# Local attention heads on full PE rows, two raw buffers instead of three, two more ring slots

## The chip, the cores and the metric

One core of one Trainium2 chip runs the whole program in one launch. The metric is device time in microseconds (us) of one execution. The engines are PE (TensorE; PEld is its weight load), DVE (VectorE), ACT (ScalarE), POOL (GpSimd) and SP (SyncE, which here only issues transfers). Three runs of the kernel before took 451.62, 452.07 and 452.42 us, median 452.07.

## The reference

Three layers follow each other. Attention has 4 batches of 8 heads, 576 tokens and 64 features a head. Heads 0 to 3 are local: a token sees itself and the 31 tokens before it. Heads 4 to 7 are strided: a token sees the earlier tokens that have the same remainder by 32. Then come a soft mixture of 8 experts with 4 slots each, and an MLP with a squared ReLU.

```python
rel = pos[:, None] - pos[None, :]
mask_local = (rel >= 0) & (rel < 32)
mask_strided = (rel >= 0) & (pos[None, :] % 32 == pos[:, None] % 32)
scores = where(mask, q @ k.T / 8, -1e9)          # softmax over keys, then @ v
logits = x @ phi                                 # x: 2304 x 512, phi: 512 x 32
slot_input = softmax(logits, axis=0).T @ x       # 32 slots
slot_out[e] = relu(slot_input[e] @ w1[e]) @ w2[e]
x = softmax(logits, axis=1) @ slot_out
out = relu(x @ w_in) ** 2 @ w_out                # 512 -> 2048 -> 512
```

`w_in` and `w_out` arrive with 8 bytes a number and are narrowed on the chip; everything else is f32.

## The kernel before

Attention runs in 16 units. A unit is two heads of one batch, and the order is `(b, p) for p in (0, 2, 1, 3)`, so that even units are local and odd units are strided. A step `u` of the loop works on several units at once: the transposes of q and k for unit u+1 (`Tk0 Tk1 Tq0 Tq1`, function `st_T`), the scores of unit u (`S`, `st_S`), exp (`E`) and the normalization of strided rows (`N`), the transposes of the probabilities of unit u-1 (`PT0 PT1`), its product with v (`A`, `st_AV`), the transposes of the result of unit u-2 (`X0 X1`), and for each batch the logits (`L`) and the slot sums (`R1 Rs R2 R3`). `PIPE` lists the order of these parts, one list for even steps and one for odd ones. Within the loop `pin` chains the instructions of PE, ACT, DVE and POOL in exactly this order, each engine by itself.

The raw q and k of a unit lie with 72 partitions. For a local unit `st_T` turns them with ordinary matmuls against the identity, 64 columns at a time, the two heads side by side in the PE array (`tile_position` (0, 0) and (0, 64)); for a strided unit it uses PE transposes of 128 columns. An eviction by ACT writes the turned q and k to `qTb` and `kTb`. Local scores take 18 blocks of 32 queries. Each block is one matmul for each head against 64 keys, head 0 on array rows 0 to 63 and head 1 on rows 64 to 127, in four groups of 32 columns. `st_AV` does the same for 20 blocks against v, 65 columns wide (the last column holds ones and gives the denominators). An f32 matmul stands in the trace as two PE instructions, a transpose as one. A second copy of v, moved down by 32 tokens, is made on the chip by `shift_v` (`vd` on DVE, `va` on ACT).

All transfers are issued by SP in one order (`load_to`). `NR` = 3 pairs of raw buffers hold q and k, so step u loads unit u+4 (`ld`); v of local units has two buffers (`lv` loads unit u+3). At the end of a step `ft` fetches two blocks of 512 KB of weights. These go to `RING` = 26 ring slots of 512 KB or, when an attention buffer has been given back (`give`), to one of the `NA` = 17 slots of the attention space (`space`). After the last step all slots are filled, and the experts' two layers (`layer1`, `layer2`) free them one by one. The MLP reads its own weights through the same ring.

Of the kernel before, what the change touches and what calls it, by code (L numbers as in the profile page):

```python
# [7 lines left out]
F32 = mybir.dt.float32  # L8
# [11 lines left out]
RING = 26  # L20
NA = 17
# [10 lines left out]
PAD = 0  # L32

@with_exitstack
def kernel(
# [271 lines left out]
    NR = 3  # L307
# [10 lines left out]
    for u in (NU - 2, NU - 1):  # L318
        qTb[u % 2], kTb[u % 2] = part(128, S), part(128, 32 + S)
# [7 lines left out]
    vS, Ps, Ts = part(128, 2, 8, D), part(128, 8, 2, 64), part(128, 8, 2, 36)  # L327
# [6 lines left out]
    def local(u):  # L334
        return units[u][1] < 2
# [16 lines left out]


    def pad(ps, n=PAD):
        for _ in range(n):
            nc.tensor.matmul(out=ps[:, 384:512], lhsT=identb, rhs=identb, start=True, stop=True)

    def shift_v(u, h, copy):
        vL = vLb[u // 2 % 2]
        copy(vL[64 * h:64 * h + 32, 1:18, 0:D], vL[64 * h + 32:64 * h + 64, 0:17, 0:D])  # L360

    def load_v(u):
# [3 lines left out]
        for h in range(2):  # L366
            src = v[b, 2 * p + h]
            if local(u):
                load_to(
                    vLb[u // 2 % 2][64 * h + 32:64 * h + 64, :, 0:D], src.rearrange("(j p) d -> p j d", p=32)  # L370
# [25 lines left out]
    load(2)  # L396
    load_to(phi_sb, phi.rearrange("(k p) s -> p k s", p=128))
    load_v(1)
    load_v(2)
# [8 lines left out]
    nc.vector.memset(kTb[0][:, 0:32], 0.0)  # L408
    diag(ident, [[-1, 128]], 0, 1.0)
    for vL in vLb:  # L410
        nc.vector.memset(vL[:, :, D:D + 1], 1.0)
        for h in range(2):
            nc.vector.memset(vL[ts(2 * h, 32), 0, 0:D], 0.0)
# [26 lines left out]
    behind(nc.gpsimd.memset(Ps, 0.0), last_diag)  # L440
# [5 lines left out]
    def st_T(u, which, halves=(0, 1)):  # L446
# [6 lines left out]
        for i in halves:  # L453
            ps = psum("t")
            if u:
                pad(ps)
            ps = ps[:, 0:288]
            for r in range(4):
                if not local(u):
                    nc.tensor.transpose(  # L460
                        out=ps[:, ts(r, 72)], in_=src[:, ts(4 * i + r, 128)], identity=ident[0:72, 0:72]
                    )
                    continue
                for h in range(2):
                    nc.tensor.matmul(  # L465
                        out=ps[ts(h, 64), ts(r, 72)], lhsT=src[:, ts(8 * h + 4 * i + r, 64)],
                        rhs=ident[0:72, 0:72], start=True, stop=True, tile_position=(0, 64 * h),
                    )
            if local(u):
                o = dst[:, 32 * which:32 * which + S].rearrange("c (p r) -> c p r", r=8)[:, :, ts(i, 4)]  # L470
                ps = ps.rearrange("c (r p) -> c p r", r=4)
            else:
                o = dst[:, ts(i, 288)]
            dve = u == 0 and i
            if which:
                ins = (nc.vector.tensor_copy if dve else nc.scalar.copy)(out=o, in_=ps)  # L476
            elif dve:
                ins = nc.vector.tensor_scalar(out=o, in0=ps, scalar1=scale, scalar2=None, op0=ALU.mult)
            else:
                ins = nc.scalar.activation(out=o, in_=ps, func=AF.Copy, scale=scale)  # L480
            if dve:
                v_first[0] = ins
# [13 lines left out]
    def st_S(u):  # L496
        qT, kT = qTs[u], kTb[u % 2]
        pss = [psum("s") for _ in range(2)]
        m = maskl.rearrange("p t w -> p (t w)") if local(u) else masks.rearrange("p n w -> p (n w)")
        n = m.shape[1]  # L500
        pad(pss[0])
# [796 lines left out]
```

## Time and profile before

| | us |
|---|---|
| median of three runs | 452.07 |
| the profiled execution | 451.3 |
| its span in the profile | 449.5 |
| PE busy | 408.5 (91%) |
| DVE busy | 252.5 (56%) |
| ACT busy | 242.0 (54%) |
| POOL busy | 62.5 (14%) |
| transfers, share of 16 DMA engines | 48.9% of the span |

[...] The span has three stages: attention from 0 to about 152 us with its last steps up to 177, the experts from there to about 214, and the MLP up to the end. The 1.8 us between the profiled execution's time and its span lie outside the instructions.

### The profile page before, as it was taken

Reading aid. Unit: us, or ns where it says so; the run is one execution under the profiler, and the core shown is the slowest. Engines: PE = TensorE matmul, PEld = TensorE weight load, DVE = VectorE, ACT = ScalarE, POOL = GpSimd, SP = SyncE. Lnnn points to the kernel's source line nnn. Section 1 sums busy time; section 2 is a strip of 40 time slices with the busy share of each in tenths; the row PEclk is TensorE's granted clock in tenths of the full one; section 3 lists DMA queues with packets and bytes.
Section 4 is the critical chain, followed back from the end, with each engine's and each line's share of the span. In section 5 each row is a group of like instructions: output and inputs, shape, how many; then the busy total and the mean of one; then the engine's idle time right before and its main releaser. Section 6 shows DMA issues by size and latency. Waiting matters only on the chain.

```text
span 449.5 us, 11728 instructions
## 1 busy us (share of the span) xinstructions
PE 408.5 (91%) x4910; PEld 316.0 (70%) x4910; DVE 252.5 (56%) x538; ACT 242.0 (54%) x532; POOL 62.5 (14%) x85
## 2 busy tenths in 40 slices
PE   7698886998788869999799998999999999999996
PEld 4677764676577555354577886888878888888884
DVE  4344554667445635311677667686867768635344
ACT  1334535265344512101688777766777677766660
POOL 3210100001101000000143114310242113300000
PEclk9999969698978958999999999999999999999999
DMA  7998668399845499999931223231200000003033
GB/s 149 197 215 247 178 189 236 112 253 240 226 153 190 148 412 359 365 410 408 362 97 50 92 93 93 71 117 49 93 0 1 0 2 0 1 1 141 23 117 141
DMA packets 31988, 70.02 MB, mean 156 GB/s; under 512 B 12608, under 2 KB 12864, under 8 KB 31936
## 3 DMA queue, kind: packets, MB, share of 16 engines
q1 hardware_dynamic: 31936, 69.28, 48.9%
q8 instruction: 38, 0.62, 0.6%
q14 instruction: 14, 0.11, 0.1%
HBM read 64.55 MB, written 4.72 MB: 154 GB/s over the span
## 4 chain that ended last, share of the span: by engine, by line
PE 74%; DMA 8%; DVE 7%; issue 5%; ACT 4%; POOL 1%; SPq 0%; DVEq 0%; POOLq 0%; ACTq 0%
PE t L1245 14%; PE s L1245 14%; PE o L1245 13%; DMA w<-in_moe_w_dram 5%; PE t L465 4%; PE t L1201 3%; PE o L617 3%; PE t L460 2%; PE o L786 2%; PE t L578 2%; DMA w<-in_moe_w_out_dram 2%; DMA space<-in_v_dram 2%; PE s L509 2%; PE s L523 2%; PE t L648 2%
## 5 line engine op out<-in xcount | busy, mean ns | idle before, releaser
L1222 DVE TENSOR_TENSOR w<-r,w 128x384 fp32r<-128x384 f32 x95 | 55.4, 583 | 71.8 <-ACT w L1208 71.0
L1245 PE MATMUL s<-w 128*128 128x512 f32 x288 | 83.0, 397 | 0.2 <-DVE part L1260 0.2
L1245 PE MATMUL t<-w 128*128 128x512 f32 x288 | 74.4, 393 | 0.0
L1245 PE MATMUL o<-w 128*128 128x512 f32 x288 | 73.7, 391 | 0.0
L1206 ACT ACTIVATE r<-t 128x384 f32<-128x384 f32 x94 | 46.2, 491 | 42.7 <-PE t L1201 36.7
L1245 PEld LDWEIGHTS o<-w 128*128 128x128 f32 x288 | 54.1, 188 | 12.4
L1245 PEld LDWEIGHTS s<-w 128*128 128x128 f32 x288 | 52.6, 188 | 11.6 <-ACT w L1097 0.6
L1245 PEld LDWEIGHTS t<-w 128*128 128x128 f32 x288 | 53.2, 188 | 10.3
L1207 ACT ACTIVATE r<-r 128x384 f32<-128x384 f32 x94 | 49.5, 526 | 2.9
L1208 ACT CAST w<-r 128x384 fp32r<-128x384 f32 x94 | 48.3, 514 | 3.5
L476 ACT COPY space<-t 128x288 f32<-128x288 f32 x31 | 11.7, 398 | 48.9 <-PE t L465 27.9
L190 POOL TENSOR_SCALAR nm<-w 128x512 f32<-128x512 f32 x28 | 21.2, 762 | 106.2 <-DMA w<-in_moe_w_out_dram 67.7
L1201 PE MATMUL t<-cT,A 128*128 128x384 f32 x96 | 32.3, 338 | 3.1 <-POOL A L1149 1.6
L1098 POOL TENSOR_TENSOR w<-wf,w 128x512 fp32r<-128x512 f32 x16 | 21.7, 1359 | 74.6 <-ACT w L1097 69.7
L465 PE MATMUL t<-ident,space 72*64 72x72 f32 x512 | 28.5, 288 | 1.6 <-DVE xNb L668 0.7
L465 PEld LDWEIGHTS t<-ident,space 72*64 72x64 f32 x512 | 25.6, 189 | 4.8 <-DVE xNb L668 1.9
L554 POOL TENSOR_TENSOR space<-space,sm 128x576 f32<-128x576 f32 x7 | 8.1, 1153 | 120.9 <-DVE sm L553 61.8
L193 DVE TENSOR_SCALAR nm<-nm 128x512 uint32<-128x512 uint32 x32 | 14.4, 449 | 16.8 <-ACT nm L188 10.2
L1201 PEld LDWEIGHTS t<-cT,A 128*128 128x128 f32 x96 | 17.9, 188 | 7.7 <-POOL A L1149 2.0
L194 DVE SCALAR_TENSOR_TENSOR nm<-w,nm 128x512 uint32<-128x512 uint32 x32 | 22.2, 692 | 1.1
L489 DVE TENSOR_REDUCE mx<-s 128x5 f32<-128x320 f32 (+1 forms) x32 | 15.0, 467 | 12.4 <-PE s L523 8.7
L523 PE MATMUL s<-space 64*36 64x36 f32 x512 | 9.0, 229 | 7.9 <-issue 7.9
(203 smaller groups left out, 564.8 us busy)
## 6 DMA issues: line engine op xcount, KB each, us to landing
w<-in_moe_w_dram SPq DMA_DIRECT2D x46, 512.0 KB
space<-in_moe_w_dram SPq DMA_DIRECT2D x18, 512.0 KB
w<-in_moe_w_in_dram SPq DMA_DIRECT2D x16, 512.0 KB
w<-in_moe_w_out_dram SPq DMA_DIRECT2D x16, 512.0 KB
space<-in_k_dram SPq DMA_DIRECT2D x16, 288.0 KB
space<-in_q_dram SPq DMA_DIRECT2D x16, 288.0 KB
out_dram<-part SPq DMA_DIRECT2D x17, 256.0 KB
space<-in_v_dram SPq DMA_DIRECT2D x16, 144.0 KB
```

The lines of the kernel that those rows point to most:

```text
L190: nc.gpsimd.tensor_scalar(out=m, in0=hf, scalar1=2.0 ** -112, scalar2=1.0, op0=ALU.mult, op1=ALU.mult)
L194: nc.vector.scalar_tensor_tensor(out=r, in0=hi, scalar=0x80000000, in1=r, op0=ALU.bitwise_and, op1=ALU.bitwise_or)
L465: nc.tensor.matmul(out=ps[ts(h, 64), ts(r, 72)], lhsT=src[:, ts(8 * h + 4 * i + r, 64)], rhs=ident[0:72, 0:72], start=True, stop=True, til ...
L489: nc.vector.tensor_reduce(out=mx[:, 0:n], in_=ps, axis=AX.X, op=ALU.max, negate=True)
L523: nc.tensor.matmul(out=pss[a][64 * h:64 * h + 36, ts(i, 36)], lhsT=qv[ts(a, 64), i, h], rhs=kv[ts(a, 64), i, h], start=False, stop=(i == 7 ...
L1098: nc.gpsimd.tensor_tensor(out=lo, in0=r, in1=hi.bitcast(F32), op=ALU.subtract)
L1201: nc.tensor.matmul(out=ps[:, 0:HB], lhsT=A4[c][:, ts(f % QF, 128)], rhs=cT4[:, c0:c0 + HB], start=True, stop=True)
L1206: nc.scalar.activation(out=r, in_=ps[:, 0:HB], func=AF.Relu)
L1207: nc.scalar.activation(out=r, in_=r, func=AF.Square)
L1208: nc.scalar.copy(out=gh, in_=r)
L1222: nc.vector.tensor_tensor(out=gl, in0=r, in1=gh.bitcast(F32), op=ALU.subtract)
L1245: nc.tensor.matmul(out=acc[t], lhsT=a[:, ts(t, 128)], rhs=wo[f][:, ts(w, 512)], start=(first and k == 0), stop=(last and k == 2),)
```

## The change

`st_T` treats local units like strided ones: PE transposes of 128 columns, which hold a pair of neighbouring tokens of one head, 4 for each half (a half is now a head). The result has even tokens on partitions 0 to 63 and odd ones on 64 to 127, so each half is evicted with two instructions of 64 partitions. For local units `kTb` becomes 128 x 2 x 608: head 0's keys stand on partitions 0 to 63 of the first plane, head 1's on 64 to 127 of the second, and the rest is zero. One matmul per block then computes both heads over all 128 rows, 128 columns wide; `vL` is laid out in the same way, so that `st_AV` needs one matmul of 130 columns per block. The two PSUM tiles of S and A now hold blocks of tokens (0 to 2 and 3 to 4 of five) instead of heads. `S` moves behind `Tk0 Tk1` in both lists. `vL` has one buffer instead of two, `Ts` shares the memory of `Tl`, `NR` is 2, `NA` is 15 and `RING` is 28. Local v is loaded by `load_v(a1 + 2)` in place of `a1 + 4`.

```diff
-RING = 26
-NA = 17
+RING = 28
+NA = 15
-    "Rs S Tk0 Tk1 X0 X1 PT0 PT1 Tq0 Tq1 ld E R2 A lv R3 vd va cv ft".split(),
-    "S Tk0 Tk1 L X0 X1 PT0 E PT1 N Tq0 Tq1 ld R1 A lv ft".split(),
+    "Rs Tk0 Tk1 S X0 X1 PT0 PT1 Tq0 Tq1 ld E R2 A lv R3 vd va cv ft".split(),
+    "Tk0 Tk1 S L X0 X1 PT0 E PT1 N Tq0 Tq1 ld R1 A lv ft".split(),
-    NR = 3
+    NR = 2
-            vLb = [part(128, 18, 65) for _ in range(2)]
-            Pl, Tl = part(128, 5, 2, 64), part(128, 5, 128)
+            vL, Pl = part(128, 18, 2, 65), part(128, 5, 2, 64)
...
     load(0)
     load(1)
     load_v(0)
-    load(2)
     load_to(phi_sb, phi.rearrange("(k p) s -> p k s", p=128))
     load_v(1)
-    load_v(2)
...
+    for t in (vL[0:64, :, 1, :], vL[64:128, :, 0, :], Ps):
+        behind(nc.gpsimd.memset(t, 0.0), last_diag)
...
             for r in range(4):
-                if not local(u):
-                    nc.tensor.transpose(
-                        out=ps[:, ts(r, 72)], in_=src[:, ts(4 * i + r, 128)], identity=ident[0:72, 0:72]
-                    )
-                    continue
-                for h in range(2):
-                    nc.tensor.matmul(
-                        out=ps[ts(h, 64), ts(r, 72)], lhsT=src[:, ts(8 * h + 4 * i + r, 64)],
-                        rhs=ident[0:72, 0:72], start=True, stop=True, tile_position=(0, 64 * h),
-                    )
+                nc.tensor.transpose(
+                    out=ps[:, ts(r, 72)], in_=src[:, ts(4 * i + r, 128)], identity=ident[0:72, 0:72]
+                )
             if local(u):
+                o = dst[:, i, 32:32 + S] if which else dst
+                o = o[ts(i, 64)].rearrange("c (p r a) -> c a p r", r=4, a=2)
+                io = [(ps[ts(a, 64)].rearrange("c (r p) -> c p r", r=4), o[:, a]) for a in range(2)]
...
-                for h in range(2):
-                    nc.tensor.matmul(
-                        out=pss[h][ts(cg, 32), ts(t, 64)],
-                        lhsT=qT[ts(h, 64), ts(qb, 32)], rhs=kT[ts(h, 64), 32 * qb:32 * qb + 64],
-                        start=False, stop=(qb + 4 >= 18), tile_position=(64 * h, 32 * cg),
-                    )
+                i = t >= 3
+                nc.tensor.matmul(
+                    out=pss[i][ts(cg, 32), ts(t - 3 * i, 128)].rearrange("p (h w) -> p h w", h=2),
+                    lhsT=qT[:, ts(qb, 32)], rhs=kT[:, :, 32 * qb:32 * qb + 64],
+                    start=False, stop=(t == 2 or qb + 4 >= 18), tile_position=(0, 32 * cg),
+                )
...
-                for h in range(2):
-                    nc.tensor.matmul(
-                        out=pss[h][ts(cg, 32), ts(t, 65)],
-                        lhsT=T[ts(h, 64), t, ts(cg, 32)], rhs=vL[ts(h, 64), min(qb, 17)],
-                        start=True, stop=True, tile_position=(64 * h, 32 * cg),
-                    )
+                i = t >= 3
+                nc.tensor.matmul(
+                    out=pss[i][ts(cg, 32), ts(t - 3 * i, 130)],
+                    lhsT=T[:, t, ts(cg, 32)], rhs=vL[:, min(qb, 17)].rearrange("p h e -> p (h e)"),
+                    start=True, stop=True, tile_position=(0, 32 * cg),
+                )
```

## Rows read from the trace of the kernel before

**Rows 1.** Windows by stage; PEclk is the granted clock, DMA share follows it.

```profile
core 0: us, PE busy (x) PEld busy (x) DVE busy (x) ACT busy (x) POOL busy (x), PEclk, DMA share, GB/s
...
28.13:48.11 19.98, 18.80 (x393) 15.96 (x388) 10.44 (x24) 8.88 (x20) 1.11 (x1) 1.00 0.83 199
...
89.39:104.58 15.19, 13.00 (x432) 10.76 (x427) 11.10 (x27) 8.64 (x22) 1.95 (x2) 1.00 0.96 254
...
152.34:214.00 61.66, 54.79 (x746) 31.14 (x745) 21.76 (x61) 11.16 (x29) 0.64 (x1) 0.89 0.98 384
214.00:449.50 235.50, 227.01 (x1118) 184.80 (x1118) 151.46 (x271) 163.24 (x333) 47.13 (x49) 1.00 0.21 73
...
28.13:142.31 114.18, 98.00 (x2487) 78.70 (x2481) 63.48 (x154) 53.33 (x137) 5.77 (x5) 0.87 0.75 199
```

**Rows 2.** PE's waits from 0 to 142.31 us: total, times, longest.

```profile
PE s L523 <- issue: 7.9, 4, 3.3
PE o L605 <- issue: 3.7, 3, 2.1
PE o L786 <- ACT nm L188: 3.0, 1, 3.0
...
PE t L460 <- issue: 1.8, 1, 1.8
...
PE s L509 <- issue: 0.9, 2, 0.5
```

**Rows 3.** The page: busy time and instructions of each engine; the instruction-loading queue.

```profile
PE 408.5 (91%) x4910; PEld 316.0 (70%) x4910; DVE 252.5 (56%) x538; ACT 242.0 (54%) x532; POOL 62.5 (14%) x85
...
q8 instruction: 38, 0.62, 0.6%
```

**Rows 4.** PE's timeline, parts at the lower clock: start, duration, line.

```profile
44.65 2.19 PE L465 MATMUL t<-ident,space 72*64 72x72 f32 x32
46.77 1.41 PE L605 MATMUL o<-space 64*32 64x65 f32 x80
...
48.75 1.34 PE L509 MATMUL s<-space 64*32 64x64 f32 x72
...
129.24 1.17 PE L460 MATMUL t<-ident,space 72*128 72x72 f32 x8
```

**Rows 5.** PE's timeline, the same parts at the higher clock.

```profile
52.25 0.67 PE L460 MATMUL t<-ident,space 72*128 72x72 f32 x8
...
88.41 1.04 PE L605 MATMUL o<-space 64*32 64x65 f32 x80
...
119.04 1.22 PE L465 MATMUL t<-ident,space 72*64 72x72 f32 x32
...
123.76 0.97 PE L509 MATMUL s<-space 64*32 64x64 f32 x72
```

**Rows 6.** PE's timeline, logits of two units at the lower clock.

```profile
61.34 0.63 PE L682 MATMUL t<-space,phi_sb 128*32 128x128 f32 x5
...
61.98 0.63 PE L682 MATMUL t<-space,phi_sb 128*32 128x128 f32 x5
```

**Rows 7.** Timeline of the first unit: v's issue, its shift, the scores.

```profile
2.51 0.90 SPq L115 DMA_DIRECT2D space<-in_v_dram  x2
...
10.69 1.10 ACT L360 COPY space<-space 32x1088 f32<-32x1088 f32 x1 [4.18 <-DMA space<-in_v_dram]
...
11.69 0.39 ACT L480 ACTIVATE space<-t 128x288 f32<-128x288 f32 x1
12.14 1.34 PE L509 MATMUL s<-space 64*32 64x64 f32 x72 [2.50 <-ACT space L480]
```

**Rows 8.** An odd step at the higher clock: Tq's wait.

```profile
102.17 0.72 PE L465 MATMUL t<-ident,space 72*64 72x72 f32 x16 [0.69 <-DVE xNb L668]
```

**Rows 9.** The page: ACT's evictions of turned k.

```profile
L476 ACT COPY space<-t 128x288 f32<-128x288 f32 x31 | 11.7, 398 | 48.9 <-PE t L465 27.9
```

**Rows 10.** SP's timeline: the last v.

```profile
149.81 2.47 SPq L115 DMA_DIRECT2D space<-in_v_dram  x4
```

More of the change, by code (lines that the diff above doesn't have):

```diff
@@ L350, in load, with shift_v @@
         raw[u] = (tq, tk)
[L354 to L360, printed above, removed]
+    def shift_v(h, copy):
+        copy(
+            vL[64 * h:64 * h + 32, 1:18, h, 0:D], vL[64 * h + 32:64 * h + 64, 0:17, h, 0:D]
+        )
     def load_v(u):
@@ L407 @@
     nc.gpsimd.memset(ident, 0.0)
-    nc.vector.memset(kTb[0][:, 0:32], 0.0)
+    nc.vector.memset(kTb[0], 0.0)
     diag(ident, [[-1, 128]], 0, 1.0)
-    for vL in vLb:
-        nc.vector.memset(vL[:, :, D:D + 1], 1.0)
-        for h in range(2):
-            nc.vector.memset(vL[ts(2 * h, 32), 0, 0:D], 0.0)
+    for h in range(2):
+        nc.vector.memset(vL[ts(h, 64), :, h, D:D + 1], 1.0)
+        nc.vector.memset(vL[ts(2 * h, 32), 0, h, 0:D], 0.0)
     nc.vector.tensor_copy(identb, ident)
@@ L481, in st_T @@
-            if dve:
-                v_first[0] = ins
+                o = dst[:, i, 32:32 + S] if which else dst
+                o = o[ts(i, 64)].rearrange("c (p r a) -> c a p r", r=4, a=2)
+                io = [(ps[ts(a, 64)].rearrange("c (r p) -> c p r", r=4), o[:, a]) for a in range(2)]
+            else:
+                io = [(ps, dst[:, ts(i, 288)])]
+            for n, (x, o) in enumerate(io):
+                dve = u == 0 and n
+                if which:
+                    ins = (nc.vector.tensor_copy if dve else nc.scalar.copy)(out=o, in_=x)
+                elif dve:
+                    ins = nc.vector.tensor_scalar(out=o, in0=x, scalar1=scale, scalar2=None, op0=ALU.mult)
+                else:
+                    ins = nc.scalar.activation(out=o, in_=x, func=AF.Copy, scale=scale)
+                if dve:
+                    v_first[0] = ins
@@ L603, in st_AV @@
                 cg, t = qb % 4, qb // 4
[L604 to L611 removed]
+                i = t >= 3
+                nc.tensor.matmul(
+                    out=pss[i][ts(cg, 32), ts(t - 3 * i, 130)],
+                    lhsT=T[:, t, ts(cg, 32)], rhs=vL[:, min(qb, 17)].rearrange("p h e -> p (h e)"),
+                    start=True, stop=True, tile_position=(0, 32 * cg),
+                )
+            for (t0, t1), ps in zip(((0, 3), (3, 5)), pss):
+                n = 2 * (t1 - t0)
+                norm(
+                    x[:, t0:t1].rearrange("p t (h d) -> p (t h) d", h=2),
+                    ps[:, 0:65 * n].rearrange("p (t e) -> p t e", e=65), n,
+                )
         else:
@@ L848 @@
     for h in range(2):
-        shift_v(0, h, (nc.scalar.copy, nc.gpsimd.tensor_copy)[h])
+        shift_v(h, (nc.scalar.copy, nc.gpsimd.tensor_copy)[h])
     nc.vector.memset(one1, 1.0)
@@ L886, in step @@
             if a1 is not None:
-                load_v(a1 + (4 if local(a1) else 2))
+                load_v(a1 + 2)
         elif what == "vd":
             if 0 < u < NU and local(u):
-                shift_v(u, 0, nc.vector.tensor_copy)
+                shift_v(0, nc.vector.tensor_copy)
         elif what == "va":
             if 0 < u < NU and local(u):
-                shift_v(u, 1, nc.scalar.copy)
+                shift_v(1, nc.scalar.copy)
         elif what == "L":
```

63 lines of the change are left out of this document (27 added, 36 removed).

## The prediction

> **What bounds the kernel now.** I read the windows by stage first. The MLP keeps PE busy for 227.0 of 235.5 us at the full granted clock, and the change puts nothing into it; the two extra ring slots only let its loads run further ahead, and a DMA share of 0.21 shows that loads are not what it lacks [rows 1]. From 152 to 214 us the experts' weights stream at a DMA share of 0.98, while PE is busy 54.8 of 61.7 us [rows 1]: transfers and PE run side by side, and both start from the end of attention. So what attention gains or loses is handed on. It is the stage to read.
>
> There PE is the bound. From unit 2's scores to unit 14's (28.13 to 142.31 us, six pairs of a local and a strided step, 19.03 us a pair) PE is busy 98.0 of 114.2 us, DVE 63.5, ACT 53.3, transfers 0.75 [rows 1]. The list of waits then says what PE's idle time is: mostly "issue", 7.9 + 3.7 + 1.8 + 0.9 = 14.3 us in ten waits of up to 3.3 us, for which no engine is named [rows 2]. I read these as waits for PE's own instructions: queue q8 carries 0.62 MB in 38 loads, and PE and PEld have 9,820 instructions, 63 bytes for each, 258 in a load [rows 3].
>
> PE's clock matters as much. [...] (The windows give 1.00 for 28.13 to 48.11, though the 2.19 us stand in that stretch; I go by the durations.) A pair took 19.98 us there and 15.19 us at the higher level [rows 1].
>
> **The change part by part.** Counted over the stage, with eight local units; a part's level is read from its duration.
>
> *Turning local q and k.* Each Tk or Tq falls from 16 matmuls (32 instructions) to 8 transposes, which is what strided units have. That is 2.19 - 1.17 = 1.02 us less at the lower clock and 1.22 - 0.67 = 0.55 at the higher one [rows 4, 5]. Of the 16 parts, nine and a half ran at the lower level: 9.5 x 1.02 + 6.5 x 0.55 = 13.3 us less. Unit 0's two (2.0 us) don't count: its scores wait for an eviction (L480) that stands on ACT behind the shift of v, and that one waits for v's transfer until 10.69 [rows 7]. 11.3 us are left.
>
> *Local scores and A.* Half as many instructions, but each streams twice the columns, and two halves of the array no longer work side by side. No row has the new form. From below: if instructions were the limit, half of them take half the time, 0.67 us less for S and 0.70 for A at the lower clock, 0.49 and 0.52 at the higher [rows 4, 5]. From above: the logits are of the new shape (128 rows, 32 columns, 128 moving, four groups), and two of their units start 0.64 us apart [rows 6]. Their first column group streams 2 x (128 + 64) = 384 columns in that time, 1.67 ns a column. The new S streams 5 x 2 x 128 = 1,280 in its first group, 2.13 us; the new A 5 x 2 x 130 = 1,300, 2.17 us; half of these at the higher clock. With the 0.07 us by which a part's last matmul overhangs, S rises by 0.86 (lower) or 0.16 (higher), A by 0.83 or 0.10. I take these, since the shape is the same: S at 4 lower and 4 higher, A at 2 and 6, gives 4.1 + 2.3 = 6.4 us more. By the other end it is 7.9 us less. Mask matmuls keep their 640 columns, and DVE's maxima and norms their elements.
>
> *Waits for instructions.* A local unit loses 124 PE matmul records (48 of T, 36 of S, 40 of A) of some 390 to 430 for a pair [rows 1]. Of 415 on average 291 remain, seven tenths, and so of the loads; the 129 records of a load last 5.9 us now (19.03 x 129 / 415) and some 2 us more then. If only the number falls, 10.0 of the 14.3 us stay; if every wait is also shortened by 2 us, about 1.5. The strided A and S, 128 instructions close together, stay as they are, so I take 5: 9.3 us less. The range is 4.3 to 12.8.
>
> [...]
>
> *New waits.* In odd steps Tq waits for a PSUM buffer that DVE empties (L668) after the maxima of S. It waits 0.69 us at the higher clock with Tk, 1.22 us, between S and X [rows 5, 8]. Now Tk comes before S and covers nothing: up to 1.2 us more per odd step, four of eight at the higher level, 4.8 us. At the lower clock the parts that remain are long enough; the bounds are 0 and 8 x 1.2 = 9.6. A is queued behind Tq on PE, and the next step behind A.
>
> *Evictions.* Each half of a local T needs two of 0.40 us where it had one [rows 9]: 8 x 4 x 0.40 = 12.8 us on ACT. ACT has room (53.3 of 114.2 us [rows 1]); the two that stand ahead of the copy on which A waits fall into the wait just charged. I take 0; if that cover is gone, 8 x 0.8 = 6.4.
>
> *Two raw buffers, one v buffer, ring.* A load of q or k has two steps to land instead of three, 15 us or more, and I cost that at nothing. The first v landed 8.2 us after its issue, behind four other loads [rows 7]; a local v now has one step, 7.6 us (half of 15.19) to 10 [rows 1]. I take 0 (rival below). Ring and space together have 43 slots as before, and two blocks a step are fetched as before, so attention prefetches no more. But the slot that the second block of step 15 gets now overlaps unit 14's v and must wait for its A; before, it lay over an idle v buffer. SP, free of v from 149.81 + 2.47 on [rows 10], may idle for 0 to 2 us; I take 1. The new zeroing on DVE and POOL lies before the first v lands [rows 7].
>
> *Sum.* -11.3 + 6.4 - 9.3 + 4.8 + 1.0 = -8.4 us on the profiled execution's 451.3: 442.9. The median lies 0.8 above that execution: 443.7. The clock's levels are taken as they fell before.
>
> **The rivals.**
>
> *The clock stays low* (slower). PE gets more idle holes at the higher level (the 1.2 us above), and transposes in place of matmuls. Of the six pairs' busy time, some 50 us ran at the higher level (19.98 us of the first pair and 0.13 x 2 x 114.2 = 30 us more did not). If these ran 1.65 times as long (between 1.22 to 2.19 and 0.97 to 1.34 [rows 4, 5]) they would cost 32 us; the new waits (4.8) go, the change's PE work is -2.04 + 0.86 + 0.83 a unit, -2.5 in all, and issue waits shrink by 12: 451.3 + 32 - 2.5 - 12 + 0.8 = 470. It is slower than before once some 13 us more than before run low (8.4 / 0.65). Against it: S and A now stream through all rows twice as long, and the drops before came beside the long waits that should go.
>
> [...] The part of X, PT and T at 52.25 that runs transposes at 0.67 us [rows 5] shows that they at least run at the higher level once it is there.
>
> *v comes late* (slower). If a local v takes 8.2 us and queues behind two blocks (1 MB at 384 GB/s, 2.7 us [rows 1]), 10.9 in all, DVE and ACT wait 3.3 us at the shift in a step of 7.6 and 0.9 in one of 10, with Tk's evictions behind them: some 15 us over seven units, 459. It decides from a landing time of one step.
>
> *The issue waits are not instructions* and stay: -8.4 + 9.3 = +0.9, 453.0.
>
> *The clock rises early.* With the long waits gone, all pairs run like the 15.19 us one, whose DMA share of 0.96 [rows 1] allows no less: 6 x (19.03 - 15.19) = 23 us, 429.
>
> **How the numbers follow.** Forecast (436 to 451, by the bounds of the waits, of S and A) 0.50; clock low 0.13; v late 0.10; issue waits stay 0.15; clock early 0.12. The range 429 to 458 leaves out the first rival and half of the second, 0.18. Within 0.2% (0.9 us) is about what a measurement can't tell from no change. Faster: 0.97 of the forecast, all of the early clock, a third of the issue rival, 0.66. Slower: clock, v, and over a third of the issue rival, 0.28. Same: 0.06.
>
> **What would show it.** Local Tk and Tq of 0.6 to 0.7 us at the higher clock, S and A of 1.1 (2.2 at the lower); if S comes near 0.5, the column reading is wrong. Issue waits before unit 14's scores near 5 us, and 8 fewer loads on q8 (8 x 124 x 2 instructions by 258). Tq waiting for L668 in odd steps by more than 1 us. L360 waiting for v at the first unit alone. Unit 14's scores near 133 us in place of 142.31, and the MLP's length unchanged; a change in it would break the argument's first step. The prediction is wrong if PE's parts run at the lower level for most of the stage.

## The result, and the profile after

The changed kernel takes **430.22 us** (median of 4 runs, 425.39 to 436.81) beside 451.85 (449.16 to 452.42, 4 runs) of the kernel before: a ratio of 0.9497, 95% interval 0.9397 to 0.9596. The forecast was 443.7 with a range of 429 to 458. The direction held and the range holds the time, but the gain is 21.6 us where 8.4 were worked out. Single runs of these kernels scatter by some 2% either way (six of e8 from 445.28 to 463.21 about 455.41), so below a single profile is read for where time goes, and medians for how much there is; medians are over all runs, ratios over the undisturbed ones, and where these were too few there is no ratio.

The profiled execution took 431.75 us (span 429.9) beside 451.3 (span 449.5). I cut both spans at the same events: the masks of unit 2's and of unit 14's scores, the first matmul of the experts' first layer, the first of the MLP.

| stretch, us | before | after | difference |
|---|---|---|---|
| start, to unit 2's scores | 28.1 | 19.1 | -9.0 |
| six pairs, to unit 14's scores | 114.2 | 108.8 | -5.3 |
| rest of attention | 34.7 | 32.7 | -2.0 |
| experts | 39.2 | 36.0 | -3.2 |
| MLP | 233.3 | 233.3 | 0 |

The windows by stage of the changed kernel answer to [rows 1]; columns are the same. The first line is the six pairs.

```profile
core 0: us, PE busy (x) PEld busy (x) DVE busy (x) ACT busy (x) POOL busy (x), PEclk, DMA share, GB/s
19.11:127.95 108.84, 83.09 (x1740) 65.71 (x1738) 62.97 (x157) 64.43 (x163) 7.01 (x7) 0.87 0.91 214
127.95:160.60 32.65, 25.87 (x444) 18.89 (x443) 17.98 (x63) 12.64 (x39) 1.08 (x1) 0.90 0.93 334
160.60:196.60 36.00, 36.00 (x428) 17.98 (x427) 10.71 (x19) 6.77 (x14) 0.67 (x1) 1.00 1.02 404
...
197.50:429.90 232.40, 224.27 (x1092) 182.53 (x1088) 149.84 (x267) 161.12 (x326) 47.21 (x49) 1.00 0.20 72
```

Before, PE was busy for 98.0 us of the six pairs and transfers for 0.75 of them. Now PE is busy 83.1, so it lost 14.9 us of work, but 9.6 us of that came back as idle time (16.2 to 25.8), and the transfers' share is 0.91. The MLP didn't move, which the first step of the prediction needed.

Next, PE's waits up to unit 14's scores (total, times, longest), which answer to [rows 2].

```profile
PE s L520 <- issue: 6.1, 1, 6.1
PE t L452 <- DVE xNb L667: 4.0, 3, 2.4
PE s L512 <- issue: 4.0, 1, 4.0
PE t L452 <- DMA space<-in_k_dram: 2.9, 4, 1.7
PE t L562 <- ACT space L464: 2.3, 3, 1.5
PE t L452 <- DMA space<-in_v_dram: 1.7, 1, 1.7
```

With 2.1 that isn't shown, "issue" is 12.2 us in four waits: fewer and longer than before. Of the rest, L667 is the wait that the prediction put down to the new order; v and L464 (ACT's evictions) are new, and k has grown from 0.6 us.

The page's counts answer to [rows 3]: 992 fewer matmul records and 7 fewer loads on q8.

```profile
PE 385.8 (90%) x3918; PEld 296.7 (69%) x3918; DVE 253.4 (59%) x538; ACT 255.6 (59%) x562; POOL 64.8 (15%) x87
...
q8 instruction: 31, 0.51, 0.5%
```

The granted clock has two values in the records of both traces, 0.50 and 1.00, below called the lower and the higher level. In the kernel before, for one, it is 0.50 from 58 to 60 us (columns as above):

```profile
58.00:60.00 2.00, 1.82 (x39) 1.75 (x41) 1.85 (x4) 0.09 (x1) 0.00 (x0) 0.50 1.08 262
```

PE's timeline (start, duration, line) shows the new parts at both levels of the clock, as [rows 4, 5] did the old ones.

```profile
9.53 2.35 PE L498 MATMUL s<-space 128*32 128x128 f32 x36
11.80 1.22 PE L452 MATMUL t<-ident,space 72*128 72x72 f32 x8
...
34.97 1.32 PE L600 MATMUL o<-space 128*32 128x130 f32 x40
36.21 0.72 PE L452 MATMUL t<-ident,space 72*128 72x72 f32 x8
...
37.14 1.29 PE L498 MATMUL s<-space 128*32 128x128 f32 x36
38.35 0.86 PE L647 MATMUL t<-ident,xNb 128*128 128x128 f32 x5
...
53.79 2.24 PE L600 MATMUL o<-space 128*32 128x130 f32 x40
55.96 1.22 PE L452 MATMUL t<-ident,space 72*128 72x72 f32 x8
```

From start to start, scores take 2.27 us at the lower level (9.53 to 11.80) and 1.21 at the higher (37.14 to 38.35), A 2.17 (53.79 to 55.96) and 1.24; a turning lasts 1.22 and 0.72.

Now the groups by line of the six pairs, busy time and mean of one (ns), then the engine's idle time before them and what ended it. First the kernel before, from 28.13 to 142.31 us:

```profile
L465 PE MATMUL t<-ident,space 72*64 72x72 f32 x384 | 20.0, 274 | 0.9 <-DVE xNb L668 0.7
L460 PE MATMUL t<-ident,space 72*128 72x72 f32 x96 | 10.6, 263 | 1.8 <-issue 1.8
L617 PE MATMUL o<-space 36*64 36x36 f32 x384 | 8.5, 249 | 0.0
L578 PE MATMUL t<-ident,space 128*128 128x128 f32 x48 | 7.8, 315 | 0.0
L605 PE MATMUL o<-space 64*32 64x65 f32 x486 | 7.3, 240 | 2.7 <-issue 2.7
L509 PE MATMUL s<-space 64*32 64x64 f32 x432 | 7.3, 267 | 0.9 <-issue 0.9
```

And the changed kernel, from 19.11 to 127.95 us:

```profile
L452 PE MATMUL t<-ident,space 72*128 72x72 f32 x195 | 19.4, 245 | 7.5 <-DVE xNb L667 4.0 <-DMA space<-in_v_dram 1.7 <-DMA space<-in_k_dram 1.7
L600 PE MATMUL o<-space 128*32 128x130 f32 x240 | 9.9, 322 | 0.0
L498 PE MATMUL s<-space 128*32 128x128 f32 x216 | 7.9, 276 | 0.9 <-issue 0.4 <-ACT space L468 0.3
L616 PE MATMUL o<-space 36*64 36x36 f32 x384 | 6.8, 224 | 0.0
L575 PE MATMUL t<-ident,space 128*128 128x128 f32 x48 | 6.5, 280 | 0.0
```

All turning fell from 30.6 to 19.4 us, scores and A rose from 14.6 to 17.8. That is -8.0 of the -14.9. The other 6.9 us fell on instructions that the change doesn't touch, such as the strided A (8.5 to 6.8) and its transposes (7.8 to 6.5): the same instructions, more of them at the higher level of the clock (of the pairs, 52.6 us before and 27.3 after were at the lower one).

Last, the chain of waits from 15 to 130 us by line, the largest shares first:

```profile
by line: DMA space<-in_v_dram 17.0%; issue 9.0%; DMA space<-in_k_dram 7.2%; PE t L452 6.6%; PE o L600 5.1%; DVE space L481 4.8%; DVE mx L477 4.1%; PE s L498 3.2%; PE t L681 3.1%; PE o L616 2.9%; DVE nm_run L714 2.8%; PE s L520 2.6%; PE t L5
...
19.09 9.24 DMA space<-in_v_dram
...
39.90 8.22 DMA space<-in_k_dram
...
56.49 10.30 DMA space<-in_v_dram
```

In this execution transfers hold a quarter of the chain: two loads of v, of 9.24 and 10.30 us, and one of k.

### The profile page after: what moved, and what is told of

Same layout as the page of the kernel before. It is cut to its first block, busy times and chain, and to the rows that moved or that the text cites. A ratio compares the mean times of both kernels' runs of the same rounds, so it can differ in the third digit from the quotient of the medians.

```text
span 429.9 us, 9774 instructions
## 1 busy us (share of the span) xinstructions
PE 385.8 (90%) x3918; PEld 296.7 (69%) x3918; DVE 253.4 (59%) x538; ACT 255.6 (59%) x562; POOL 64.8 (15%) x87
## 4 chain that ended last, share of the span: by engine, by line
PE 70%; DVE 11%; DMA 9%; ACT 4%; issue 3%; POOL 1%; SPq 0%; DVEq 0%; ACTq 0%; POOLq 0%
PE t L1244 15%; PE s L1244 14%; PE o L1244 14%; DMA space<-in_v_dram 5%; PE t L1200 4%; PE t L1052 4%; PE o L1022 3%; DMA space<-in_k_dram 3%; PE t L452 2%; DMA space<-in_q_dram 2%; PE o L785 2%; PE o L616 2%; DVE space L481 2%; PE o L600 1%; PE t L681 1%
## 5 line engine op out<-in xcount | busy, mean ns | idle before, releaser
L1244 PEld LDWEIGHTS s<-w 128*128 128x128 f32 x288 | 52.6, 188 | 11.5 <-ACT w L1096 0.7
L452 PE MATMUL t<-ident,space 72*128 72x72 f32 x256 | 26.6, 254 | 9.4 <-DVE xNb L667 4.0
L452 PEld LDWEIGHTS t<-ident,space 72*128 72x128 f32 x256 | 22.4, 160 | 15.7 <-DVE xNb L667 6.8
L1200 PEld LDWEIGHTS t<-cT,A 128*128 128x128 f32 x96 | 17.9, 188 | 7.8 <-POOL A L1148 2.0
L464 ACT COPY space<-t 64x288 f32<-64x288 f32 (+1 forms) x46 | 18.3, 409 | 6.1 <-PE t L452 5.5
L468 ACT ACTIVATE space<-t 64x288 f32<-64x288 f32 (+1 forms) x46 | 18.7, 423 | 5.0 <-PE t L452 4.7
L477 DVE TENSOR_REDUCE mx<-s 128x8 f32<-128x288 f32 (+2 forms) x32 | 15.0, 467 | 10.6 <-PE s L498 5.8
L192 DVE TENSOR_SCALAR nm<-nm 128x512 uint32<-128x512 uint32 x32 | 14.4, 449 | 11.6 <-ACT nm L187 7.0
```

The source lines that it names most:

```text
L452: nc.tensor.transpose(out=ps[:, ts(r, 72)], in_=src[:, ts(4 * i + r, 128)], identity=ident[0:72, 0:72])
L468: ins = nc.scalar.activation(out=o, in_=x, func=AF.Copy, scale=scale)
L1200: nc.tensor.matmul(out=ps[:, 0:HB], lhsT=A4[c][:, ts(f % QF, 128)], rhs=cT4[:, c0:c0 + HB], start=True, stop=True)
L1244: nc.tensor.matmul(out=acc[t], lhsT=a[:, ts(t, 128)], rhs=wo[f][:, ts(w, 512)], start=(first and k == 0), stop=(last and k == 2),)
```

## The experiments

The table puts all kernels side by side. "Low" is the time up to the MLP at the lower clock, from the trace's records of each change of level (the time before the first record is counted as low, which the durations of the parts there bear out: a turning of 2.19 us at 44.65 before, scores of 2.35 at 9.53 after). "Same 1,328" is the busy time of seven groups of PE instructions that every one of these kernels has in the same number and form: strided A and scores, the transposes of strided and local probabilities and of strided x, the logits. "Clock" is the mean granted clock of all runs of a kernel. The kernel before ran beside each group of experiments, on three chips: medians 453.57 (13 runs), 450.51 (11) and 455.45 (11), 453.18 over all 35. The profiled executions of e6 and e8 are the longest of their runs, so their stretches read long. "Low", the busy time and the stretches come from one execution of each kernel; "clock" and median come from all its runs and weigh more. The changed kernel ran beside the kernel before in the result alone, so a difference of under some 5 us between it and an experiment, as between these medians, can be one of the chips.

| kernel | PE records to the MLP | low, us | same 1,328, us | clock | unit 2's scores at | six pairs, us | median, us |
|---|---|---|---|---|---|---|---|
| before | 3,806 | 94 | 61.9 | 0.916 | 28.1 | 114.2 | 453.2 |
| e1 buffers | 3,806 | 109 | 65.4 | 0.918 | 24.8 | 113.8 | 450.2 |
| e8 shift behind | 3,806 | 121 | 66.1 | 0.906 | 24.2 | 122.9 | 455.4 |
| e4 turning | 3,422 | 87 | 60.0 | 0.924 | 17.9 | 116.4 | 443.1 |
| e9 full rows | 3,198 | 76 | 56.4 | 0.940 | 26.2 | 106.1 | 439.1 |
| e5 old turning | 3,198 | 62 | 56.5 | 0.949 | 23.8 | 103.3 | 438.7 |
| e10 A half | 3,134 | 56 | 58.0 | 0.935 | 23.9 | 100.9 | 433.8 |
| e11 S half | 3,102 | 66 | 56.7 | 0.933 | 21.8 | 100.1 | 435.3 |
| after | 2,814 | 47 | 55.7 | 0.955 | 19.1 | 108.8 | 430.2 |
| e3 S first | 2,814 | 57 | 56.5 | 0.940 | 18.9 | 105.4 | 434.1 |
| e2 three raw | 2,814 | 69 | 54.4 | 0.936 | 19.5 | 104.6 | 436.8 |
| e6 two v | 2,814 | 70 | 59.0 | 0.948 | 23.5 | 110.0 | 429.4 |
| e12 both | 2,814 | 63 | 59.3 | 0.930 | 21.5 | 111.4 | 441.6 |
| e7 one block | 2,814 | 53 | 54.0 | 0.948 | 20.5 | 94.5 | 438.0 |

**e1: the buffers alone.**

```diff
-RING = 26
-NA = 17
+RING = 28
+NA = 15
...
-    NR = 3
+    NR = 2
...
-    load(2)
```

> The kernel before with the buffers of the change alone: two raw buffers, NA 15, RING 28, no early load of unit 2's q and k. Its PE program and its two buffers of v are those of before. Theory A (the gain comes from PE's parts: fewer columns in T, shorter waits): 450 to 452 us, unit 2's scores near 28 us, transfers' share in the six pairs 0.75. Theory B (the gain comes from what is loaded when: less ahead of the first unit, weights earlier): 440 to 445 us, unit 2's scores 3 to 5 us earlier, at 23 to 25 us.

Measured: 450.18 us (445.0 to 459.34, 10 runs) beside 453.57, with unit 2's scores at 24.8. Two raw buffers cost nothing and two more ring slots bring at most a few us, which the scatter doesn't let me tell from nothing. The gain isn't here: the time is theory A's, though unit 2's scores come where theory B has them.

**e2: the changed kernel with three raw buffers.**

```diff
-RING = 28
-NA = 15
+RING = 26
+NA = 17
...
-    NR = 2
+    NR = 3
...
+    load(2)
```

> The changed kernel with three raw buffers, NA 17 and RING 26 as before, and unit 2's q and k loaded ahead of the loop; v keeps one buffer. Theory A: 429 to 431 us, as changed. Theory B: 436 to 441 us, since unit 2's 576 KB stand ahead of the loads of v again.

Measured: 436.8 us (428.08 to 442.23, 4 runs), beside 453.57. A third raw buffer doesn't help; whether it costs something stays inside the scatter. The time is in theory B's range, but unit 2's scores come at 19.5 us, as early as without the third buffer, so B's cause doesn't show.

**e4: the turning alone, in the kernel before.** Order, scores, A and buffers stay.

```diff
-                for h in range(2):
-                    nc.tensor.matmul(
-                        out=ps[ts(h, 64), ts(r, 72)], lhsT=src[:, ts(8 * h + 4 * i + r, 64)],
...
+                nc.tensor.transpose(
+                    out=ps[:, ts(r, 72)], in_=src[:, ts(4 * i + r, 128)], identity=ident[0:72, 0:72]
+                )
```

> The kernel before with local q and k turned by transposes of token pairs (two evictions each half), everything else as before: S and A of two heads side by side, three raw buffers, S ahead of Tk. Theory A: 13.3 us less PE work and 384 fewer PE records of 916: 436 to 441 us. Rival (transposes keep the clock low): 452 us or more, PE's parts of the six pairs mostly at the lower level. Rival (PE's work was not what counted, the order and the loads were): 447 to 452.

Measured: 443.09 us (438.26 to 444.71, 4 runs), ratio 0.9731, interval 0.9627 to 0.9835. The time lies just above theory A's range and below both rivals'. Unit 2's scores come at 17.9 us, 10 earlier than before; the six pairs, with less work, are no shorter. The list of PE's waits up to unit 14's scores gives a part of the reason:

```profile
PE s L503 <- issue: 9.5, 3, 5.8
PE s L517 <- issue: 5.1, 2, 3.4
```

With 6.3 more that isn't shown, 20.9 us of "issue" where the kernel before had 14.8 (the ten waits of [rows 2], and one of 0.5 before the logits), though q8 made 18 loads up to there instead of 22.

**e5: the changed kernel with the old turning.**

```diff
-                nc.tensor.transpose(
-                    out=ps[:, ts(r, 72)], in_=src[:, ts(4 * i + r, 128)], identity=ident[0:72, 0:72]
-                )
+                for h in range(2):
+                    nc.tensor.matmul(
+                        out=ps[ts(h, 64), ts(r, 72)], lhsT=src[:, ts(8 * h + 4 * i + r, 64)],
...
```

> The changed kernel with local q and k turned by ordinary matmuls as before (each half evicted by two instructions, one a head); S and A on full rows, S behind Tk, two raw buffers. Theory A: the 11 to 13 us of T come back: 440 to 444 us. Rival (S and A with half the instructions carry the gain by shortening the waits for instructions): 430 to 434 us.

Measured: 438.65 us (435.4 to 442.88, 4 runs), ratio 0.9644, interval 0.9564 to 0.9725. This was the surprise: everything but the turning, which by my sum takes back a part of the gain, is worth some 15 us by itself. The time lies between the two theories.

**e3: the changed kernel with the scores ahead of Tk.**

```diff
-    "Rs Tk0 Tk1 S X0 X1 PT0 ...
-    "Tk0 Tk1 S L X0 X1 PT0 ...
+    "Rs S Tk0 Tk1 X0 X1 PT0 ...
+    "S Tk0 Tk1 L X0 X1 PT0 ...
```

> After, with the scores of a unit put back ahead of the first turning of the next (Tk) in both steps' orders; all else as after. Theory A (the order is a small part: it costs PE a wait for L667 in odd steps, 4.0 us in three waits before unit 14's scores, and gains nothing that the traces show): these waits go, 426 to 430 us, unit 2's scores still near 19 us. Rival B (the order carries the gain that I did not forecast, since Tk ahead of S lets loads and evictions run earlier): 436 to 445, and unit 2's scores come later than 22 us.

Measured: 434.14 us (428.81 to 438.01, 6 runs), ratio 0.9593, interval 0.9521 to 0.9665, and unit 2's scores at 18.9. The time lies between the two theories; the start is as early as A has it, so the order carries neither the start nor most of the gain. But the wait for L667, which I had put down to the order, is still there up to unit 14's scores:

```profile
PE t L452 <- DVE xNb L667: 4.6, 3, 2.3
```

**e6: the changed kernel with two buffers of v.**

```diff
-RING = 28
-NA = 15
+RING = 26
+NA = 17
...
+    load_v(2)
...
-                load_v(a1 + 2)
+                load_v(a1 + (4 if local(a1) else 2))
```

> After, with two buffers of local v again, each loaded two steps earlier, and the ring two slots smaller for it. Theory A (v lands late in its one step: DVE and ACT wait 13.3 and 13.2 us for it, and some 8 to 10 of it reach PE, the scores of odd steps queueing behind the shift): these waits go to under 3 us, PE's idle time in the six pairs falls from 25.7 to about 17, 420 to 424 us, if what PE then does isn't held elsewhere. Rival B (v is late because the transfers are full, at a share of 0.91; an earlier v only makes q, k or the experts' blocks later): the waits move to q and k, 428 to 432.

Measured: 429.35 us (422.05 to 438.12, 6 runs), ratio 0.9476, interval 0.9368 to 0.9585: the same as the changed kernel. In the changed kernel DVE and ACT waited for v like this (0 to 131 us):

```profile
DVE space L355 <- DMA space<-in_v_dram: 13.3, 4, 5.4
ACT space L355 <- DMA space<-in_v_dram: 13.2, 5, 4.4
```

With two buffers DVE doesn't wait for v any more, and ACT for 0.8 us. But now PE waits for k (PE's waits, then the chain from 15 to 130 us):

```profile
PE t L456 <- DMA space<-in_k_dram: 15.3, 7, 3.9
PE s L524 <- issue: 2.9, 2, 2.1
...
by line: DMA space<-in_k_dram 41.3%; PE t L456 9.4%; PE o L605 6.5%; PE t L686 5.2%; PE s L524 5.1%; issue 4.6%; PE t L665 2.2%; PE t L566 2.2%; PE s L502 2.1%; PE o L621 2.1%; PE s L516 1.9%; PE t L652 1.8%; PE t L579 1.8%; PE o L790 1.8%;
```

Rival B holds: the wait moved from v's queue place to k's. (The trace is that of the longest run, 438.12 us, so the size of the wait for k is not that of a usual run.)

**e7: the changed kernel, one of the experts' blocks fetched in a step instead of two.**

```diff
-                fetch(2)
+                fetch(1)
```

> After, with one of the experts' blocks fetched in a step instead of two; attention asks for 8 MB less, which the experts' stage must then load after it. Theory A (attention is now held by transfers: v, q and k queue behind two blocks a step): transfers' share in the six pairs falls from 0.91 to under 0.75, PE's idle time from 25.7 to under 16, unit 14's scores come at 116 to 122 us instead of 127.95; the experts' stage grows by up to 16 blocks of 0.5 MB at 384 GB/s, 22 us, so 434 to 446 in all. Rival B (the idle time is PE's wait for instructions, whatever the transfers do): unit 14's scores stay at 126 to 130, idle time 23 to 27, and the whole becomes 445 to 452.

Measured: 438.04 us (435.76 to 439.6, 6 runs), ratio 0.9766, interval 0.9709 to 0.9824. The windows of its six pairs and of its experts' stage:

```profile
20.50:115.00 94.50, 81.89 (x1740) 64.62 (x1739) 62.91 (x155) 64.34 (x162) 7.02 (x7) 0.89 0.66 178
151.80:201.00 49.20, 45.08 (x427) 20.00 (x426) 10.66 (x19) 6.86 (x14) 0.65 (x1) 0.96 1.03 408
```

With a share of 0.66 the six pairs take 94.5 us, the shortest of all, with 12.6 us of idle time; the issue waits are 4.4 us though q8 made the same 15 loads up to unit 14's scores as in the changed kernel. Theory A holds on this side. On the other, the experts' stage must load what attention left out: 49.2 us at a share of 1.03, 13 longer. Transfers, then, hold a part of attention in the changed kernel, but taking them out of it gives nothing in the end: the interval of the ratio lies wholly above the changed kernel's (0.9397 to 0.9596).

**e8: the kernel before, with ACT's shift of the first v behind unit 0's last eviction.**

```diff
...
+        ins = shift_v(0, h, (nc.scalar.copy, nc.gpsimd.tensor_copy)[h])
+        if h == 0:
+            behind(ins, a_last[0])
```

> Before, with one edge added: ACT's shift of unit 0's v stands behind its last eviction of unit 0's turned q, so that unit 0's scores don't wait for v's transfer. Theory A (the first 28 us are long because the first scores wait behind that shift, and the rest of the stage then runs at the same pace): unit 0's scores at 9.5 to 10.5 instead of 12.14, unit 2's at 24 to 26, 449 to 451 us. Rival B (the early scores are what brings the clock up at 13 us and not at 50): unit 2's scores near 19 to 21 and 440 to 445 us. Rival C (the start of after comes from its fewer matmuls alone): no change, 452 to 454, unit 2's scores near 28.

Measured: 455.41 us (445.28 to 463.21, 6 runs) beside 450.51 (445.9 to 464.46, 11 runs): no gain. PE's timeline of the start:

```profile
7.79 0.96 PE L511 MATMUL s<-space 64*32 64x64 f32 x72 [0.28 <-DVE space L478]
...
16.30 0.34 PE L525 MATMUL s<-space 64*36 64x36 f32 x6 [3.52 <-issue]
16.57 2.19 PE L465 MATMUL t<-ident,space 72*64 72x72 f32 x32
...
19.95 2.19 PE L465 MATMUL t<-ident,space 72*64 72x72 f32 x32
```

Unit 0's scores start at 7.79 us instead of 12.14 [rows 7], earlier than theory A's 9.5 to 10.5: the step does what it should. Unit 2's come at 24.2 instead of 28.1, but e1, with the instructions of PE and the shift as before, has 24.8, so this second difference may be one between single executions. At the end nothing of it shows, and no kernel with the old turning has unit 2's scores before 23.8 us. The start, with two parts of the turning of 2.19 us each, stays long.

**e9: full rows alone.** The kernel before with the new scores and A, with the one v buffer that their layout leaves room for; old turning (the matmuls of e5, two evictions each), three raw buffers, scores first. Against e5 the edit is

```diff
-RING = 28
-NA = 15
+RING = 26
+NA = 17
...
-    "Rs Tk0 Tk1 S X0 X1 PT0 ...
+    "Rs S Tk0 Tk1 X0 X1 PT0 ...
...
-    NR = 2
+    NR = 3
...
```

> Before, with the new forms of local scores and A alone (full rows, pairs of tokens, and the one v buffer that their layout leaves room for): the old turning, three raw buffers, scores first. Theory A (the full-row forms carry most of what I did not forecast: PE runs for less time at the lower clock, about 60 us of the 200 before the MLP where the kernels with half rows had 87 to 121): 436 to 442 us, low time of 50 to 75 us, masks to logits of the pairs 98 to 104 us. Rival B (by the columns these forms cost 6.4 us, and the gain came from turning and order): 451 to 460, low time of 90 us or more.

Measured: 439.05 us (433.25 to 445.12, 6 runs), ratio 0.9722, interval 0.9628 to 0.9816. Its groups by line, 0 to 200 us:

```profile
L459 PE MATMUL t<-ident,space 72*64 72x72 f32 x512 | 25.8, 270 | 3.1 <-DVE xNb L677 2.1 <-DMA space<-in_q_dram 0.6 <-DMA space<-in_k_dram 0.3
...
L610 PE MATMUL o<-space 128*32 128x130 f32 x320 | 14.3, 332 | 2.5 <-issue 1.1 <-DVE space L578 1.0 <-ACT space L577 0.4
L508 PE MATMUL s<-space 128*32 128x128 f32 x288 | 12.4, 313 | 4.3 <-DVE space L476 4.3
L454 PE MATMUL t<-ident,space 72*128 72x72 f32 x128 | 11.9, 242 | 0.0
```

The same groups of the kernel before, also 0 to 200 us:

```profile
L465 PE MATMUL t<-ident,space 72*64 72x72 f32 x512 | 28.5, 288 | 1.6 <-DVE xNb L668 0.7 <-DMA space<-in_k_dram 0.6
L460 PE MATMUL t<-ident,space 72*128 72x72 f32 x128 | 14.1, 267 | 1.8 <-issue 1.8
...
L605 PE MATMUL o<-space 64*32 64x65 f32 x640 | 10.0, 246 | 5.1 <-issue 3.7 <-DVE space L571 1.1 <-ACT space L570 0.4
L509 PE MATMUL s<-space 64*32 64x64 f32 x576 | 9.7, 267 | 3.9 <-ACT space L480 2.5 <-issue 1.4
```

The new forms cost what the columns said: 26.7 us for 19.7, 7.0 more (6.4 forecast). And yet the kernel is faster. The turning, with the same instructions, fell from 42.6 to 37.7, the seven unchanged groups from 61.9 to 56.4. The time at the lower clock fell from 94 to 76 us, issue waits up to unit 14's scores from 14.8 to 10.9. Theory A's time came; its low time and its pairs (106.1 us) lie just past what it allowed.

**e10 and e11: one of the two forms put back to half rows.** e10 has A, e11 has the scores in the old form, all else as changed.

```diff
-                    out=pss[i][ts(cg, 32), ts(t - 3 * i, 130)],
-                    lhsT=T[:, t, ts(cg, 32)], rhs=vL[:, min(qb, 17)].rearrange("p h e -> p (h e)"),
+                        out=pss[h][ts(cg, 32), ts(t, 65)],
+                        lhsT=T[ts(h, 64), t, ts(cg, 32)], rhs=vL[ts(h, 64), min(qb, 17), h],
...
```

```diff
-                    lhsT=qT[:, ts(qb, 32)], rhs=kT[:, :, 32 * qb:32 * qb + 64],
+                        lhsT=qT[ts(h, 64), ts(qb, 32)], rhs=kT[ts(h, 64), h, 32 * qb:32 * qb + 64],
...
```

> After, with local A alone put back to half rows (40 matmuls of 65 columns for 20 of 130). Theory A (both full-row forms hold the clock): low time before the MLP between after's 47 us and the 87 us of the kernel that has half rows and the new turning, 433 to 438 us. Rival B (the scores alone hold it): as after, 427 to 432 us, or better by the 2.6 us that A's columns cost in the pairs. Rival C (A alone holds it): 440 to 446 us with a low time over 80 us.

> After, with the local scores alone put back to half rows (36 matmuls of 64 columns for 18 of 128). Theory A (both full-row forms hold the clock): low time between 47 and 87 us, 433 to 438 us. Rival B (the scores alone hold it): 440 to 446 us with a low time over 80 us. Rival C (A alone holds it): as after, 427 to 432 us.

Measured: e10 433.81 us (430.86 to 444.61, 6 runs), ratio 0.966, interval 0.9579 to 0.9741, low time 56 us; e11 435.34 us (428.88 to 441.25, 6 runs), ratio 0.9646, interval 0.9544 to 0.9748, low time 66 us. By time and by low time both fall where theory A put them, with the low time under the 87 us of e4, which has neither form. But the intervals of the ratios reach the changed kernel's, and the low times are those of one execution each (e2 and e6, with both forms, have 69 and 70), so how the two forms share in it is not shown.

**e12: two buffers of v and three of raw q and k.** Against e6:

```diff
-RING = 26
-NA = 17
+RING = 24
+NA = 19
...
-    NR = 2
+    NR = 3
...
+    load(2)
```

> After, with two buffers of local v and three of raw q and k, four ring slots fewer in their place (the blocks that can be ahead stay 43). It may beat both kernels. Theory A (attention is limited by what the transfers move; single late buffers only decide where the wait shows): the waits for v, q and k before unit 14's scores fall under 3 us in all, but the transfers' share up to the MLP stays at 0.88 to 0.93 and the time at 427 to 433 us. Rival B (the waits themselves are the loss): 419 to 425 us, and unit 14's scores at 118 to 122 us.

Measured: 441.55 us (440.05 to 446.14, 6 runs), ratio 0.9896, interval 0.9808 to 0.9983. It is slower than the changed kernel, outside what either theory gave. Waits for v, q and k on PE come to 5.1 us, after 15.9 in e6, but the changed kernel itself has 5.2; the transfers' share in the pairs is 0.94. Issue waits are 14.4 us, with the same 15 loads of instructions that left 2.9 in e6. None of the versions beats the changed kernel by more than the scatter.

## Why the prediction was right, and its size wrong

The range held the time by luck: the median lies 1.2 us above its lower end, and two of the four runs (425.39 and 428.69) lie below it. The direction had a sound reason in part: of the two edits that carry the gain, I had the turning with its size and the full rows with the wrong sign.

**PE is the bound, in attention.** Right for the kernel before; half right after. In the changed kernel a quarter of the chain is transfers, and e7 shows that fewer of them shorten the pairs by 14 us.

**Turning.** Forecast: 13.3 us less, of which the 2.0 of unit 0 don't count. In the six pairs turning fell by 11.2 us, strided parts included, partly because more of it ran at the higher clock (a transpose's mean fell from 263 ns at L460 to 245 at L452). The kernel with the turning alone (e4) gains 10.5 us. What I mis-sized is the start. I took unit 0's share out, since the shift of v on ACT holds unit 0's scores back. In the changed kernel two of the evictions that unit 0's scores need (L468) stand ahead of that shift (L355) on ACT, and the scores start at 9.53:

```profile
7.03 0.90 ACT L468 ACTIVATE space<-t 64x288 f32<-64x288 f32 x2 [0.94 <-PE t L452]
...
10.08 1.10 ACT L355 COPY space<-space 32x1088 f32<-32x1088 f32 x1 [1.06 <-DMA space<-in_v_dram]
```

Unit 2's come at 17.9 to 23.9 us in the nine kernels with the transposes and at 23.8 to 28.1 in the five without. In e8 the place of the shift alone brings nothing that shows at the end.

**Scores and A.** The column reading was right: 2.27 and 1.21 us for scores, 2.17 and 1.24 for A, where I had 2.13 and 2.17 and half of these. No run shows an exact half at the higher clock: the scores took 0.53 of their longer time there, A 0.57. e9 paid 7.0 us more for 6.4 forecast. (The other end was added up wrongly: by its own parts it is 9.2 us less, not 7.9. The sum that gives the time doesn't use it.) But this cost is not the whole effect: the sum has the two forms 6.4 us slower, and e9 is 14 us faster. With e4's 10.5 that makes some 25 us for the two edits by themselves, and the changed kernel gains 21.6; buffers and order aren't needed for it.

**"The clock's levels are taken as they fell before."** This is the step that failed. The two full-row forms cost PE 7 us and the kernel with them alone is 14 us faster than the 453.2 of the kernel before (16 than its neighbours). Time at the lower clock before the MLP is 87 to 121 us in the four kernels with half rows in both, 47 to 76 in the ten with a full-row form; the same 1,328 instructions take 60.0 to 66.1 us in the first group and 54.0 to 59.3 in the second; and the mean granted clock over all runs is 0.906 to 0.924 in the first and 0.930 to 0.955 in the second. Over 35 runs of the kernel before, a run with a clock 0.01 higher is 2.1 us shorter (a fitted line, correlation -0.78, which by itself doesn't say which of the two makes the other). As an estimate from this line, 0.916 to 0.955 makes 8 us of the 21.6, and 0.916 to 0.940 makes 5 of e9's 14. The instructions that the change leaves alone agree with it: they took 6.9 us less in the six pairs. I had the clock as two rivals: it stays low (0.13), it rises early (0.12, 429 us). The second is the nearer to what came, but by another way: the long issue waits, which I named as its cause, didn't go.

The records of the levels say a little more. Up to unit 14's scores the clock falls about as often in both groups, 5.0 and 5.7 times a kernel; but a stretch at the lower level after a fall lasts 11.4 us on average in the four kernels with half rows (20 falls) and 6.2 us in the ten others (57 falls). The kernels' own means overlap a little, 7.7 to 17.1 and 4.6 to 9.6 us, and each is from one execution. In these executions, then, the clock doesn't fall less often with the new forms; it comes back sooner. Nor does PE's idle time alone explain it: PE idled 16.2 us of the pairs before and 25.8 in the changed kernel. The first rise scatters from one execution to the next: it comes at 50.0 us in the kernel before, at 26.8 in e1, whose instructions for PE are the same, and at 13.1 in the changed kernel.

What in these forms goes with the higher level stays open. They change several things at once (fewer instructions, all rows in use, other waits beside them), and e10 and e11 take them back together, form by form. A kernel that changes one of them alone wasn't run.

My first rival had the clock low beside transposes in the place of matmuls. e4 makes this exchange and changes nothing else on PE: it has 87 us of low time where the kernel before has 94, and a mean clock of 0.924 beside 0.912 on the same chip. No loss shows here.

**Waits for instructions.** Forecast: 14.3 us to 5. It is 12.2 in the profile of the changed kernel, but over the kernels with 15 loads up to unit 14's scores it is 2.1 (e2), 2.9 (e6), 4.4 (e7), 12.0 (e3), 12.2 (after) and 14.4 (e12). The number of loads falls as worked out (31 for the 30 forecast); the length of a wait doesn't follow it. The mean of the six is 8.0 us, some 6 less than before and inside the 4.3 to 12.8 of the prediction. So the term is not refuted as an average, but it can't be counted on in one kernel, and my rule "fewer loads, and each more often covered" is not shown.

That they are waits for instructions, which I had only inferred from the totals of q8, the traces do show. Up to unit 14's scores the 14 kernels have 83 waits without a releaser, 159 us in all, and every one of them ends 1.2 to 1.9 us after a 16 KB load on q8 has ended. So the rival "the issue waits are not instructions" falls. In the changed kernel a wait is longer the later its load starts: 0.4 us where the load starts 2.1 us before PE goes idle, 1.7 us with 0.8 us before, 4.0 with 1.2 us after, and for the one of 6.1 us, from 84.10, the load starts 3.1 us after PE has gone idle and takes 1.4 us, and PE goes on 1.65 us after that. Why it starts late isn't shown. Of the 15 loads 4 held PE up.

**New waits.** The wait for L667 has the size forecast (4.0 us for 4.8) but not the cause: e3 puts the scores back ahead of Tk, and the wait is still there, 4.6 us.

**Evictions at nothing.** ACT's busy time in the pairs rose from 53.3 to 64.4 us, 11.1 of the 12.8 worked out for all eight units, and PE waited 3.2 us for L464's evictions. Small, and not nothing.

**v in one step.** My rival priced its lateness at 15 us. It came: DVE and ACT wait 13.3 and 13.2 us, and v is 17.0% of the chain. But e6 shows that it isn't v's single buffer that costs: without it k comes late, for the same time.

**Sum.** To unit 14's scores I had 9.4 us less, and 14.4 came. After them I had 1.0 more for a ring slot, and 5.2 less came: the first matmuls of the experts no longer fall at the lower clock (in the kernel before until 179.7, by the clock's records), and transfers run at shares of 0.93 and 1.02 where they had 0.82 and 0.97. So I can place the missing 11.2 us of the profile, 5 up to there and 6.2 behind. Of the 14.4 the start gave 9.0 and the pairs 5.3; the sum's parts, laid out by where they stand, make some 2.6 and 6.8 (in the start: unit 2's turning, unit 0's scores and A, a quarter of the issue waits). So the surplus lies in the start, and by the first rise above some of it may belong to this one execution of the kernel before. By cause, some 8 of the medians' 21.6 go with the clock, by the estimate above; how the rest divides among the start, the waits and the transfers, the scatter doesn't let me say.

## What to carry to other kernels

An edit that makes a PE-bound stage's instructions fewer and fuller can pay although it streams more columns (e9 paid 7.0 us for its new forms and was 14 us faster): price its own columns, but price the granted clock of everything around it too, on a group of instructions that both kernels share. Where two resources run side by side, a gain on the one can surface as waits on the other (14.9 us of PE's work went, 9.6 us came back as idle time); here a second buffer then only chose whose name the wait carried. And before a difference of 1% is explained, see how far runs of one kernel lie apart (445.9 to 464.46 us on one chip).

## What the runs showed of the hardware

- The same 1,328 PE instructions took from 54.0 to 66.1 us before the MLP, most of all in the two kernels with the longest time at the lower clock (109 and 121 us).
- Waits without a releaser before a block of matmuls came to 2.1 and to 14.4 us with the same 15 loads of instructions; all 83 of them in 14 kernels end 1.2 to 1.9 us after such a load.
- After a fall the clock stayed at its lower level for 11.4 us on average in the four kernels with half rows and for 6.2 us in the ten with a full-row form, with about as many falls a kernel.
- A load of 144 KB of v in packets of 256 bytes stood 9.24 and 10.30 us on the chain of the changed kernel, where the first v of the kernel before had 8.2 us to its landing [rows 7].
- The same kernel on one chip ran from 445.9 to 464.46 us, with a mean clock of 0.946 at 445.93 and of 0.878 at 463.26; time and clock go against each other over its 11 runs, though not run by run (0.915 at 445.9).
